# A spectral filter and a low-rank mixer on one core: two batches turned on TensorE, a split store, and small work moved between engines

## The chip, the core and the metric

The kernel runs on one core of a Trainium2 chip. Its engines work side by side, each through its own list in order: TensorE (PE in the profile) multiplies matrices and writes to PSUM, VectorE (DVE), ScalarE (ACT) and GpSimd (POOL) work on vectors, and SyncE (SP) only issues transfers. DVE and ACT can read PSUM[...]. Transfers between DRAM and on-chip memory run on 16 DMA engines; SP, ACT and POOL queue them. The metric is the device time of one execution in microseconds (us); lower is better.

## The reference

For each of 8 batches of 3136 tokens by 256 features the program filters along the tokens in the frequency domain, then mixes. It is, shortened:

```python
X = np.fft.rfft(x, axis=1)
y = np.fft.irfft(X * (filt_r + 1j * filt_i)[None], n=3136, axis=1)
h = y.transpose(0, 2, 1) @ U @ V               # rank 32, along the tokens
u = y + h.transpose(0, 2, 1)
out = u + np.maximum(u @ w_ch1, 0.0) @ w_ch2   # 256 -> 1024 -> 256
```

Inputs and outputs are f32; the kernel works in f16 and accumulates in f32.

## The kernel before

The length is split as 3136 = 64 x 49, so that the transform becomes small matrix products with constant matrices. **Stage 1** (`st1`) is 25 products of x with `wf`, a 64-point transform; its result goes to DRAM (`ct1`) and comes back regrouped as `a2` (eight tiles, k = 0 to 7, of 98 rows by 4 x 256). **Stage 2** is two matmuls of 512 columns for each k with `w2t`. Its result is multiplied by the filters, `fb` and `fc`, three element-wise products and one sum (`mul`, with `ta`, `tb`, `y`). **Stage 3** is two matmuls with `g3`; its result is evicted to `esb` and stored to DRAM (`ct2`). **Stage 4** (`stage4`) reads it back as `e2` in chunks of 8 of the 49 residues, with the low-rank term in 32 extra rows (`put_h`), and multiplies by `sv`; the result `ut` is the mixer's input, turned. `mm1` multiplies by the first weight `w1sb` (ReLU on ACT into a ring of 17 `h` tiles), `mm2_part` by the second, `w2sb`, and `residual` adds `ut` back.

From the main loop on the work is written as **groups** of 512 tokens, six for each batch, each of eight steps: a step has one `mm1` of the group and a quarter of a `mm2` of the group before, and stage 4 of the next group stands at steps 2 and 6. Everything else is placed by an order written out by hand: `plan` holds what follows a step, `early` what precedes it. `plan_mid` places stages 2 and 3 of the next batch, `plan_rest` its low-rank part and the loads of `e2`, `plan_st1` stage 1 of the batch after that. One PSUM bank (tag `e`) serves stage 3 there, and one pair of banks stage 2.

What lies ahead of the main loop is called the preamble here. Batch 0 cannot be hidden behind another, and so has its own form: `turned` (L295) computes stage 1 with x as the stationary operand, so that the result comes out turned, into `cm`, which is laid over `fc`; `turn_a2` (L358) turns it back on TensorE with eight transposes for each k, without DRAM. `mid_first` (L354) does stages 2 and 3 with **doubled matrices**: each half of a k takes two matmuls of 512 columns in stage 2 and two in stage 3, but one single product of 1024 columns, since real and imaginary parts stand twice. Of its 16 products four (L397, j = 7, 9, 12, 14) are GpSimd's, after a copy out of PSUM on ACT; twelve (L400) are DVE's. After it come the low-rank part (L416), all of stage 1 of batch 1 (L266), and stage 4 of group 0; `make_fa` (L541) then derives the operands `fa` (laid over `fb`) and `fc` for the three-product form. In batch 1 k = 1, 3 and 5 are multiplied by GpSimd (`pooled`, L636), in later batches k = 2 and 5.

Loads that change f32 to f16 are queued on POOL, in this order: U, x of batch 0, 21 filter pieces, V, the first weight, x of batch 1, the second weight. SP loads `wf` and `s4`, stores, and reads back. Within one queue a transfer that waits holds up all behind it. `keep_warm` issues matmuls whose result nobody reads.

## Time and profile before

| | |
|---|---|
| median of 8 runs | 556.46 us (555.63 to 561.68) |
| profiled execution, its own time | 556.53 us |
| span of its instructions | 554.7 us |
| TensorE busy | 515.5 us, 93% of the span |
| ACT, DVE, GpSimd busy | 390.8, 352.9, 282.6 us |
| mean granted TensorE clock | 0.982 of full speed |
| first product of batch 0 (L400) | 25.41 us |
| first `mm1` of batch 0 (L488) | 60.90 us |
| first `mm1` of batch 1 | 134.63 us |

In the profile, `L488 PE MATMUL` is an instruction of line 488 on TensorE; `out<-in` names tiles. In a list in order of time each line has start and length in us, engine, line, operation, operands and count, and in brackets the idle time of the engine before it with what ended it. A line of waits reads: who waited for whom, us in total, times, longest. The page's `PEclk` row has 40 equal slices of the span; its digits are tenths of the full TensorE clock.

### The profile page before, as it was taken

How to read it: one execution, taken by the hardware profiler on the slowest of the kernel's cores; microseconds unless marked ns; L12 is line 12 of the kernel's file. 1: busy time of each engine (PE TensorE's matmuls, PEld its weight loads, DVE VectorE, ACT ScalarE, POOL GpSimd, SP SyncE). 2: the span in 40 equal slices, each digit the busy share in tenths (PEclk: the TensorE clock that was granted, in tenths of full speed). 3: DMA queues.
4: the chain of work that ended last, by engine and by line, in shares of the span. 5: the costliest groups of instructions: out<-in, count | busy, mean ns of one | idle time of the engine just before them, and what ended most of it. 6: DMA issues, size and time to landing. Idle time of an engine off the chain costs nothing.

```text
span 554.7 us, 11638 instructions
## 1 busy us (share of the span) xinstructions
PE 515.5 (93%) x4491; PEld 374.4 (67%) x4491; DVE 352.9 (64%) x409; ACT 390.8 (70%) x684; POOL 282.6 (51%) x194
## 2 busy tenths in 40 slices
PE   4977599986999999999999999999999999999996
PEld 2634266664767777677776777777776777777775
DVE  6764776755756785758846785758746887643332
ACT  8566868774777688767777788677767677765663
POOL 5688279951893165915683185807563287300000
PEclk8799989999999999999999999999999999999999
DMA  9998886895779468775879469765654554333212
GB/s 191 159 158 176 235 161 184 211 225 135 180 186 248 126 179 196 171 194 151 193 219 220 123 173 229 166 201 154 182 170 123 141 166 121 106 113 115 96 77 87
DMA packets 85432, 92.06 MB, mean 166 GB/s; under 512 B 6741, under 2 KB 69416, under 8 KB 85376
## 3 DMA queue, kind: packets, MB, share of 16 engines
q1 hardware_dynamic: 67968, 75.12, 46.0%
q0 software_dynamic: 16960, 15.91, 19.2%
q8 instruction: 35, 0.57, 0.4%
q10 hardware_dynamic: 448, 0.28, 0.3%
q14 instruction: 21, 0.17, 0.1%
HBM read 57.42 MB, written 49.77 MB: 193 GB/s over the span
## 4 chain that ended last, share of the span: by engine, by line
PE 64%; POOL 5%; DVE 3%; ACT 2%; issue 1%; ACTq 0%; POOLq 0%; DVEq 0%
PE psum L521 24%; PE psum L488 23%; PE psum L352 3%; PE psum L344 3%; PE psum L497 3%; PE psum L477 3%; PE psum L266 2%; POOL y L634 2%; DVE tb L632 1%; PE psum L416 1%; POOL x L170 1%; POOL tb L632 1%; POOL ta L628 1%; POOL tb L630 1%; DVE ut L482 1%
## 5 line engine op out<-in xcount | busy, mean ns | idle before, releaser
L492 ACT ACTIVATE hring<-psum 128x512 f16<-128x512 f32 (+1 forms) x416 | 237.7, 576 | 102.3 <-PE psum L488 101.1
L488 PE MATMUL psum<-ut,w1sb 128*128 128x512 f16 (+1 forms) x832 | 240.9, 371 | 3.5 <-ACT hring L492 1.7
L521 PE MATMUL psum<-w2sb,hring 128*128 128x256 f16 x1536 | 230.7, 273 | 0.0
L634 POOL TENSOR_TENSOR y<-ta,tb 128x1024 f16<-128x1024 f16 x56 | 120.6, 2160 | 159.6 <-DVE tb L632 125.1
L521 PEld LDWEIGHTS <-hring 128*128 128x128 f16 x1536 | 143.3, 98 | 62.4 <-issue 2.6
L482 DVE CAST ut<-psum 128x512 f16<-128x512 f32 x96 | 71.0, 740 | 105.4 <-PE psum L477 85.9
L488 PEld LDWEIGHTS <-w1sb 128*128 128x128 f16 x832 | 104.7, 145 | 26.1 <-issue 9.5
L529 DVE COPY och<-psum 128x512 f32<-128x512 f32 x96 | 66.2, 689 | 47.6 <-PE psum L497 46.9
L326 ACT CAST esb<-psum 98x512 f16<-98x512 f32 x128 | 74.8, 587 | 22.1 <-PE psum L344 16.4
L273 ACT CAST asb<-psum 128x512 f16<-128x512 f32 x78 | 45.8, 589 | 14.0 <-PE psum L266 12.9
L628 DVE TENSOR_TENSOR ta<-psum,fb 128x1024 f16<-128x1024 f32 x41 | 49.9, 1218 | 8.9 <-PE psum L352 8.0
L497 PE MATMUL psum<-idn,ut 128*128 128x128 f16 x392 | 53.9, 219 | 0.0
L477 PEld LDWEIGHTS <-e 96*128 96x128 f16 x768 | 35.5, 98 | 24.7 <-issue 9.3
L630 DVE TENSOR_TENSOR tb<-psum,fc 64x1024 f16<-64x1024 f32 x41 | 50.3, 1226 | 0.9
L632 DVE TENSOR_TENSOR tb<-psum,fc 64x1024 f16<-64x1024 f32 x41 | 49.9, 1218 | 0.8
L477 PE MATMUL psum<-sv,e 96*128 96x64 f16 x768 | 38.4, 193 | 5.9 <-DMA e<-ct 3.1
L344 PE MATMUL psum<-y,g 128*98 128x512 f16 x105 | 39.9, 380 | 2.7 <-POOL y L634 1.2
L497 PEld LDWEIGHTS <-ut 128*128 128x128 f16 x392 | 38.4, 98 | 4.8
L352 PE MATMUL psum<-a,w2t 98*128 98x512 f16 x113 | 34.7, 383 | 3.4 <-DMA a<-ct 2.4
L628 POOL TENSOR_TENSOR ta<-pc,fb 128x1024 f16<-128x1024 f16 x15 | 32.4, 2159 | 10.2 <-ACT pc L638 10.1
L266 PE MATMUL psum<-x,wf 128*128 128x256 f16 x168 | 31.1, 272 | 4.2 <-DVE ut L482 1.8
L630 POOL TENSOR_TENSOR tb<-pc,fc 64x1024 f16<-64x1024 f16 x15 | 31.9, 2125 | 1.2
(93 smaller groups left out, 370.8 us busy)
## 6 DMA issues: line engine op xcount, KB each, us to landing
out_dram<-och SPq DMA_DIRECT2D x47, 512.0 KB
ct<-esb SPq DMA_DIRECT2D x64, 196.0 KB
x<-in_x_dram POOLq DMA_DIRECT2D x48, 256.0 KB, 7.9
e<-ct SPq DMA_DIRECT2D x48, 256.0 KB
a<-ct SPq DMA_DIRECT2D x56, 196.0 KB
ct<-asb SPq DMA_DIRECT2D x42, 256.0 KB
wf<-wf SPq DMA_DIRECT2D x3, 256.0 KB
w1sb<-in_moe_w_ch_dram POOLq DMA_DIRECT2D x1, 512.0 KB, 7.0
```

The costliest lines, as they stand in the source:

```text
L326: nc.scalar.copy(esb[b, k][:, 2 * half:2 * half + 2, :].rearrange("p s d -> p (s d)"), pe[0:98])
L477: nc.tensor.matmul(pu[:, 64 * i:64 * i + 64], e2[b, c][:, i, 128 * dh:128 * dh + 128], sv[:, 64 * r:64 * r + 64], start=(i == 0), stop=Tru ...
L482: nc.vector.tensor_copy(o, v)
L488: nc.tensor.matmul(ph[:, 0:n], w1sb[:, dh, :, t], gr.ut[:, dh, 0:n], start=(dh == 0), stop=(dh == 1))
L492: nc.scalar.activation(h[:, 0:n], ph[:, 0:n], RELU)
L497: nc.tensor.matmul(o[:, dh * 128:dh * 128 + 128], gr.ut[:, dh, t0:t0 + n], idn, start=False, stop=(dh == 1), skip_group_check=True)
L521: nc.tensor.matmul(o, gr.h[tt][:, i * 128:(i + 1) * 128], w2sb[:, tt, :], start=(tt == 0), stop=False, skip_group_check=True)
L529: nc.vector.tensor_copy(gr.och[:, 2 * y:2 * y + 2, :].rearrange("p j d -> p (j d)"), gr.pc)
L628: eng.tensor_mul(ta, p, va)
L630: eng.tensor_mul(tb[0:64], p[64:128], vb[64:128])
L632: eng.tensor_mul(tb[64:128], p[0:64], vb[0:64])
L634: nc.gpsimd.tensor_add(ys[k], ta, tb)
```

## The change

It has these parts.

- **Layout.** Only 49 + 15 + 49 = 113 rows are used where 128 were (`NZ`), `fb` is zeroed in rows 32 to 63 alone, on DVE, and `cm` has a tile of its own. `tb` becomes three fixed tiles with zeroed middle rows.
- **Constants.** `wf` is loaded at half width and spread on DVE by two multiplications with a 0/1 column. U is loaded by SP as f32. `s4` and `kr` follow the first store.
- **mid_first.** Fifteen products are DVE's, one (j = 11) GpSimd's. Stage 3 follows two j behind. The low-rank matmuls are spread over it, and `make_fc` for k = 4 to 7 runs on ACT in it.
- **The last store.** The store of k = 7 is cut in four by rows: 0-8 (SP) and 49-57 (ACT queue), on which chunk 0 of `e2` depends, then 8-49 and 57-98. Chunk 0 is loaded in three pieces.
- **Batch 1.** Its stage 1 is `turned` like batch 0's; k = 0 and 1 are turned back ahead of the main loop, k = 2 to 7 at steps 1, 3, 7, 11, 15, 17. k = 0 to 3 use the doubled matrices (`two_q`, `mul_q`, `three_q`), k = 4 to 7 the three products, all on DVE. Stage 3 of batch 1 ends at step 37 instead of 40.
- **GpSimd's queue.** After the filters: V, x of batch 1, the copy into `sv`, the first weight, the j = 11 product; the second weight waits for chunk 0 of `e2` (by a copy of one element) and is written in pieces of 256 elements into rows of 264. `make_fc` for k = 0 to 3 and `make_fa` are 49-row copies on GpSimd; `make_neg` is DVE's.
- **x.** Of batch 3 it is loaded at steps 30, 38, 43, 45.

```diff
-    wf = np.zeros((128, 25, 128))
+    wf = np.zeros((128, 25, 64))
     for h in range(2):
-        wf[h::2, 0:24, 64 * h:64 * h + 64] = t1[:, 24 * h:24 * h + 24]
-    wf[0:64, 24, 0:64] = t1[:, 48]
+        wf[h::2, 0:24] = t1[:, 24 * h:24 * h + 24]
+    wf[0:64, 24] = t1[:, 48]
+
+    pair = np.zeros((128, 2), np.float32)
+    pair[0::2, 0] = pair[1::2, 1] = 1.0
...
-    wf = cst.tile([128, 25, 128], F16, name="wf")
-    for c in range(4):
-        i = slice(8 * c, min(8 * c + 8, 25))
-        nc.sync.dma_start(wf[:, i], wf_d.rearrange("p (i m) -> p i m", m=128)[:, i])
+
+    usb = hflat[0:64, 0:2 * NR * RANK].bitcast(F32)
+    nc.sync.dma_start(usb, moe_U.rearrange("(q r) p -> q (r p)", q=NQ))
+    wfc = hflat[:, 6272:6272 + 1604]
+    nc.sync.dma_start(wfc, wf_d)
+    wf = cst.tile([128, 24, 128], F16, name="wf")
+    wl = cst.tile([64, 64], F16, name="wl")
...
-    zero = cst.tile([128, 64], F16, name="zero")
-    nc.vector.memset(zero, 0.0)
-    nc.vector.memset(fb[96:128], 0.0)
-    nc.scalar.copy(fb[32:64].rearrange("p s (k f) -> p (s k) f", f=64),
-                   free(zero, 32, 64, 0, [[0, NK * DM // 64], [1, 64]]))
-    nc.vector.memset(fc[:, 24:29, :], 0.0)
-    usb = hflat[0:64, 0:NR * RANK]
-    nc.gpsimd.dma_start(usb, moe_U.rearrange("(q r) p -> q (r p)", q=NQ))
+    nc.vector.memset(fb[32:64], 0.0)
+
+    cm = cst.tile([128, 7232], F16, name="cm")
+    nc.vector.memset(cm[:, 2 * SEQ:], 0.0)
...
+    ud = hflat[0:64, 3136:6272].rearrange("q (p c r) -> q p c r", c=2, r=NR)
+    for p, eng in ((0, nc.vector.tensor_copy), (16, nc.scalar.copy)):
+        eng(ud[:, p:p + 16], bass.AP(tensor=usb.tensor, offset=usb.offset + p,
+                                     ap=[list(usb.ap[0]), [1, 16], [0, 2], [RANK, NR]]))
+    for h in range(2):
+        nc.vector.tensor_scalar_mul(wf[:, :, 64 * h:64 * h + 64],
+                                    wfc[:, 0:1536].rearrange("p (i m) -> p i m", m=64),
+                                    wfc[:, 1600 + 2 * h:1602 + 2 * h].bitcast(F32))
+    nc.vector.tensor_copy(wl, wfc[0:64, 1536:1600])
+    tbs = [cst.tile([NZ, 4 * DM], F16, name=f"tb_{i}") for i in range(3)]
+    for t in tbs:
+        nc.vector.memset(t[32:64], 0.0)
...
+    def turn_back(k, tag, dst, eng):
+        z = bank(tag).bitcast(F16)
+        for i in range(4):
+            for hh in range(2):
+                nc.tensor.transpose(z[:, DM * i + 128 * hh:DM * i + 128 * hh + 128],
+                                    free(cm, 0, 128, SEQ * hh + 4 * k + i, [[32, 128]]), idn)
+        (nc.vector.tensor_copy if eng is nc.vector else nc.scalar.copy)(dst, z[0:98])
...
+    def store3(b, k, p0, p1, eng=nc.sync):
+        eng.dma_start(dram(ct2[b], (4 * k * 98 + p0) * DM, [[DM, p1 - p0], [98 * DM, 4], [1, DM]]),
+                      esb[b, k][p0:p1])
...
+    fa = fb
+
+    def make_fc(k, copy):
+        copy(fc[0:NR, 4 * k:4 * k + 4], fb[64:NZ, 4 * k:4 * k + 4])
+
+    def make_neg(k):
+        nc.vector.tensor_scalar_mul(fc[64:NZ, 4 * k:4 * k + 4], fb[64:NZ, 4 * k:4 * k + 4], -1.0)
+
+    def make_fa(k):
+        nc.gpsimd.tensor_copy(fa[64:NZ, 4 * k:4 * k + 4], fb[0:NR, 4 * k:4 * k + 4])
+        if k == 7:
+            nc.gpsimd.tensor_copy(fa[64:65, 31, :], fc[0:1, 31, :])
+            for p in (0, 64):
+                nc.gpsimd.memset(fc[p:p + 1, 31, :], 0.0)
...
+        ph = psum[:, 1, 0:DM]
+
+        def low_rank_part(k):
+            for i in range(4):
+                a = 4 * k + i
+                nc.tensor.matmul(ph[32 * i:32 * i + 32], uh[:, a, :], esb[0, k][:, i, :],
+                                 start=(k == 0), stop=(k == 7), skip_group_check=True)
+
+        whole = []
 
         def do3(j, uv):
             pe = bank("e0")
             stage3(pe, [(uv[:, 0], 2, 4), (uv[:, 1], 3, 5)], j == 15)
-            out3(0, j // 2, j % 2, pe)
-
-        for k in range(4):
+            while whole and j > 3:
+                low_rank_part(whole.pop(0))
+            k = j // 2
+            out3(0, k, j % 2, pe)
+            if ndone[0, k] == 2:
+                whole.append(k)
+                if k == 0:
+                    nc.sync.dma_start(sv[0:64], s4_d)
+                    nc.sync.dma_start(kr, kr_d)
+                if k == 6:
+                    load_e2(0, 0, 40, 0)
+                if k == 7:
+
+                    store3(0, 7, 0, 8)
+                    store3(0, 7, 49, 57, nc.scalar)
+                    load_e2(0, 0, 56, 40)
+                    load_e2(0, 0, 64, 56)
+                    store3(0, 7, 8, 49)
+                    store3(0, 7, 57, 98)
...
+        for k in range(2):
             turn_a2(k)
         for c in range(4):
             load_x(1, c)
-        nc.gpsimd.dma_start(w2sb, moe_w_ch2.rearrange("(cc t) e -> cc (t e)", t=8))
+        nc.gpsimd.tensor_copy(sv[64:96, :].rearrange("p (r q) -> p r q", q=NQ),
+                              vnat.rearrange("p (q r) -> p r q", q=64))
+        nc.gpsimd.dma_start(w1sb, moe_w_ch1.rearrange("(h dd) c -> dd h c", h=2))
...
-            fin = free(fb, 0, 128, 2 * j * DM, [[0, 2], [1, 2 * DM]])
-            if j in (7, 9, 12, 14):
-                pc = sb.tile([128, 2, 2 * DM], F16, tag="pc", bufs=2, name="pc")
-                nc.scalar.copy(pc, pz)
-                uv = sb.tile([128, 2, 2 * DM], F16, tag="y", bufs=3, name="uv")
+            fin = free(fb, 0, NZ, 2 * j * DM, [[0, 2], [1, 2 * DM]])
+            uv = sb.tile([NZ, 2, 2 * DM], F16, tag="y" if j == 11 else "ta", bufs=3, name="uv")
+            if j == 11:
+                pc = sb.tile([NZ, 2, 2 * DM], F16, tag="pc", bufs=2, name="pc")
+                nc.scalar.copy(pc, pz[0:NZ])
                 nc.gpsimd.tensor_mul(uv, pc, fin)
             else:
-                uv = sb.tile([128, 2, 2 * DM], F16, tag="ta", bufs=3, name="uv")
-                nc.vector.tensor_mul(uv, pz, fin)
-            if j < 4:
-                turn_a2(j + 4)
-            todo.append((j, uv))
-            if len(todo) > 3:
-                do3(*todo.pop(0))
-        while todo:
-            do3(*todo.pop(0))
-
-
-    h1 = {}
+                nc.vector.tensor_mul(uv, pz[0:NZ], fin)
+            if j in (6, 8, 10, 12):
+                make_fc(j // 2 + 1, nc.scalar.copy)
+            if j < 6:
+                turn_a2(j + 2)
+            todo.append((j + (4 if j == 11 else 2), j, uv))
+            for t in sorted(todo):
+                if t[0] <= j or j == 15:
+                    do3(*t[1:])
+                    todo.remove(t)
+        low_rank_part(7)
+        h1[0] = hp = sb.tile([128, DM], F16, tag="hp", bufs=1, name="hp")
+        nc.vector.tensor_copy(hp, ph)
...
     keep_warm(10)
-    u_hat()
+    turned(0, 0)
+    u_hat(0, 8)
+    keep_warm(2)
+    turned(0, 1)
+    u_hat(16)
+    keep_warm(2)
+    for c in (2, 3):
+        turned(0, c)
+    u_hat(24)
+    mid_first()
+    gens = {}
+
+    def step1(b):
+        if b not in gens:
+            gens[b] = st1(b)
+        next(gens[b])
+
+    low_rank_end(0)
+    put_h(0, 0)
+    nc.gpsimd.tensor_copy(w2sb[64:65, 0, DM:DM + 1], e2[0, 0][64:65, 0, 0:1])
+    nc.gpsimd.dma_start(w2sb[:, :, 0:DM], moe_w_ch2.rearrange("(cc t) e -> cc t e", t=8))
+    for k in range(4):
+        make_fc(k, nc.gpsimd.tensor_copy)
     for c in range(4):
-        turned(c)
-        keep_warm(2)
-    nc.sync.dma_start(sv[0:64], s4_d)
-    nc.sync.dma_start(kr, kr_d)
-    mid_first()
-    load_e2(0, 0)
-    load_e2(0, 1)
-    nc.gpsimd.tensor_copy(sv[64:96, :].rearrange("p (r q) -> p r q", q=NQ),
-                          vnat.rearrange("p (q r) -> p r q", q=64))
-    low_rank(0)
-    for n, _ in enumerate(st1(1)):
-        if n == 3:
-            low_rank_end(0)
-        if n == 6:
-            put_h(0, 0)
-    load_e2(0, 2)
-    load_e2(0, 6)
-    keep_warm(6)
-    stage4(groups[0], 0)
-    stage4(groups[0], 1)
+        turned(1, c)
     for c in (1, 2, 6):
-        put_h(0, c)
-    make_fa(0)
-    make_fa(1)
+        load_e2(0, c)
+    a2q = {}
+
+    def turn_1(k, tag, eng):
+        a2q[k] = sb.tile([98, 4 * DM], F16, tag="a2", bufs=4, name="a2")
+        turn_back(k, tag, a2q[k], eng)
+
+    turn_1(0, "f0", nc.vector)
+    turn_1(1, "f0", nc.scalar)
+    for k in range(4, 8):
+        make_neg(k)
+    keep_warm(4)
+    for dh in range(2):
+        stage4(groups[0], dh)
+    put_h(0, 1)
...
+        def two_q(k, half):
+            box[k, half] = [psum[:, 5:7, :]]
+            for f in range(2):
+                stage2(psum[:, 5 + f], w2t[:, 128 * f:128 * f + 128],
+                       w2t[:, 256 + 128 * f:384 + 128 * f],
+                       a2[k][:, 2 * half * DM:2 * half * DM + 2 * DM], (k, half) == (7, 1))
+
+        def mul_q(k, half):
+            uv = sb.tile([NZ, 2, 2 * DM], F16, tag="ta", bufs=3, name="uv")
+            nc.vector.tensor_mul(uv, box[k, half][0][0:NZ],
+                                 free(fb, 0, NZ, (4 * k + 2 * half) * DM, [[0, 2], [1, 2 * DM]]))
+            box[k, half].append(uv)
+
+        def three_q(k, half):
+            uv = box[k, half][1]
+            pe = bank("e")
+            stage3(pe, [(uv[:, 0], 2, 4), (uv[:, 1], 3, 5)], (k, half) == (7, 1))
+            out3(b, k, half, pe)
+
         end = 0
-        for k in range(8):
+        if b == 1:
+
+            for j, q in enumerate((4, 6, 7, 8, 10, 11, 12, 14)):
+                at(q, two_q, j // 2, j % 2)
+                early[q + 1].append((mul_q, (j // 2, j % 2)))
+                at(q + 2, three_q, j // 2, j % 2)
+        else:
+            for k in range(3):
+                at(later(s, -6 if b == 2 else -9), fetch, k)
+        for k in range(4 if b == 1 else 0, 8):
+            if b > 1 and k + 3 < 8:
+                at(s, fetch, k + 3)
             at(s, two, k)
-            if k + 3 < 8:
-                at(s, fetch, k + 3)
             if k in on_pool:
...
-    at(1, make_fa, 2)
-    at(3, make_fa, 3)
+    for n, c in ((9, 2), (9, 6)):
+        at(n, put_h, 0, c)
+    for n, k, eng in ((1, 2, nc.vector), (3, 3, nc.vector), (7, 4, nc.scalar), (11, 5, nc.vector),
+                      (15, 6, nc.scalar), (17, 7, nc.vector)):
+        at(n, turn_1, k, "e", eng)
 
     def x_after(b):
 
         for c in range(4):
-            load_x(b, c, groups[0].h[3] if c == 0 else None)
-
-    at(4, x_after, 2)
+            load_x(b, c, groups[0].h[1] if c == 0 else None)
+
+    at(2, x_after, 2)
+    for c in range(4):
+        at((30, 38, 43, 45)[c], load_x, 3, c)
+    for k in range(4):
+        at(k, make_neg, k)
+    for k in range(4, 8):
+        at(2 * k - 4, make_fa, k)
+    for k in range(4):
+        at(2 * k + 18, make_fa, k)
     for b in range(1, NB):
         if b == 2:
-            plan_st1(b, 12, (0, 1, 3, 4, 5, 7))
+            plan_st1(b, 14, (0, 1, 3, 4, 5, 7))
         elif b > 2:
             plan_st1(b, later(start[b - 1], -60))
-        m = later(start[b - 1], (5, -9, -12)[min(b, 3) - 1])
-        z = plan_mid(b, m, (2, 5) if b > 1 else (1, 3, 5))
+        m = later(start[b - 1], (16, -9, -12)[min(b, 3) - 1])
+        z = plan_mid(b, m, (2, 5) if b > 1 else ())
```

## The prediction

> **What bounds the kernel now.** I read the page's engine rows first, then the stretches by batch, then waits and instructions in order of time inside the two stretches that are not full.
>
> ```profile
> span 554.7 us, 11638 instructions
> PE 515.5 (93%) x4491; PEld 374.4 (67%) x4491; DVE 352.9 (64%) x409; ACT 390.8 (70%) x684; POOL 282.6 (51%) x194
> PEclk8799989999999999999999999999999999999999
> ```
>
> TensorE (PE) is the bound overall, but its clock is cut early on. Busy time by stretch (columns: length, then PE, PEld, DVE, ACT, POOL busy, clock, DMA share, GB/s):
>
> ```profile
> 0.00:60.90 60.90, 42.74 (x313) 25.88 (x313) 36.69 (x45) 40.20 (x47) 39.94 (x50) 0.89 0.96 179
> 60.90:71.17 10.27, 6.52 (x41) 3.29 (x37) 9.24 (x17) 8.12 (x10) 4.65 (x8) 0.83 0.82 210
> 71.17:134.63 63.46, 55.12 (x464) 38.74 (x463) 40.61 (x45) 43.33 (x78) 42.75 (x26) 0.97 0.80 183
> 134.63:199.00 64.37, 62.88 (x562) 46.34 (x561) 42.60 (x49) 48.51 (x92) 35.47 (x22) 1.00 0.70 179
> 258.49:554.70 296.21, 289.13 (x2603) 216.59 (x2601) 182.16 (x210) 206.16 (x378) 126.03 (x69) 1.00 0.54 151
> ```
>
> The cuts are where the first `mm1` of a batch starts. From 134.63 on PE is 98% busy, and the change leaves that work alone. What can move is the preamble (60.9) and batch 0's window (73.7, of which PE is busy 61.6). Their landmarks, in order of time:
>
> ```profile
> 25.41 3.48 DVE L400 TENSOR_TENSOR uv<-psum,fb 128x1024 f16<-128x1024 f32 x3
> 39.88 0.66 PE L344 MATMUL psum<-uv,g 128*98 128x512 f16 x2 [3.28 <-POOL uv L397]
> 50.27 0.31 SPq L329 DMA_DIRECT2D ct<-esb  x1
> 53.85 1.10 SPq L438 DMA_DIRECT2D e<-ct  x2
> 60.90 0.41 PE L488 MATMUL psum<-ut,w1sb 128*128 128x512 f16 x1
> 68.00:72.00 4.00, 3.77 (x16) 1.64 (x16) 3.63 (x8) 2.07 (x4) 3.49 (x6) 0.50 0.98 203
> ```
>
> The first product is at 25.4, one of PE's three waits for GpSimd products is 3.28, the last `esb` leaves at 50.27, and SyncE may read it back only at 53.85: a store needs 3.6 us to land. The last line is again a stretch: with the clock at 0.50, 16 matmuls fill PE for 3.77 us, so a busy PE there is half a PE. In batch 0's window the waits are
>
> ```profile
> PE psum L477 <- DMA e<-ct: 3.1, 1, 3.1
> PE psum L352 <- DMA a<-ct: 2.4, 2, 1.5
> ```
>
> the first at its end (batch 1's first `e`), the second where batch 1's stage 2 waits for stage 1 to come back from DRAM.
>
> **What the skill says.** "DMA: Bandwidth & Descriptors", section "Why a DMA increments its semaphore by 16 and not by 1": a transfer queued by SyncE runs on the largest number of engines up to 16 that divides its rows, always the lowest-numbered ones, each writing one completion. The trace agrees on the number: SyncE's queue has 4,368 packets of 4 bytes, exactly 14 for each of its 120 98-row transfers and 16 for the 168 others. "TensorE: Matmul & The Clock Gate", "What's actually happening": after an idle window of some 3.4 us the clock halves. The trace agrees: half rate for 6.8 us from 67.6. "VectorE: DVE Perf Modes", "The perf-mode tier table": a product from PSUM runs at 1x; here 1.22 us for 1,024 elements, on 128 as on 64 partitions, so 113 partitions gain nothing.
>
> **S1, start to first product.** U comes as f32 by SyncE (+0.2 MB), `wf` at half width (-0.4), `s4` after the first store (-0.4): 0.6 MB less before the last x. At the 189 GB/s of the first 20 us that is 3.1 us; x lands at 16.5 instead of 19.6. The lag from there to the product was 5.8. Removed: ACT's 7.0 us zero fill. Added on DVE: two scaled copies of `wf`, three memsets, about 2.6 us, under the x loads. First product 22.0.
>
> **S2, mid_first.** Before: 25.41 to 50.24, with 4.6 of PE waits for GpSimd. After: DVE has 15 products x 1.22 + a 0.69 copy = 19.0; ACT has 6 turns x 1.01 + 16 evictions x 0.59 + 4 `make_fc` at about 1.0 (half of 1.89 for twice the columns) + 1.01 = 20.6, beginning 1.5 earlier. The one GpSimd product waits for the 6.97 us `sv` copy but has four slots. I take 21.5: last `esb` at L = 43.5. x of batch 1 lands by 42.5 (shifted as above, `s4` in, `w1sb` out), in time.
>
> **S3, L to the first mm1.** Before 10.7, with stage 1 of batch 1 in it. After: low-rank end and `put_h` 2.6; seven DVE evictions of batch 1's turn x 0.69 4.7; turn back 0.6 and copy 0.7, with latencies 1.5; four `make_neg` x 0.37 (half of 0.69) 1.5; `ut` 0.75; second stage 4 0.35. Sum 11.4: first `mm1` at 54.9, 6.0 earlier.
>
> **S4, batch 0's window.** PE was busy 61.6, of which 3.4 is the half clock; 58.2 at full rate. Added: six turns back x 8 transposes x 0.0725 = 3.5, and 16 more 512-column matmuls x 0.217 = 3.5 by the doubled matrices. Gone: the wait for `a`, and the wait for `e` at the end, since the last stage 3 stands at step 37 instead of 40. DVE has 8 products of the doubled kind and 12 others for batch 1, 20 x 1.22 = 24.4, where it had 15 (18.3), since three k were GpSimd's; it loses the eight 0.69 passes of `make_fa` (5.5), so it stays near 51 of 73, off the bound unless the `two`/`mul` pair shares its PSUM buffer step by step, when each product (1.22) must fit into a step (about 1.3). GpSimd drops nine products of 2.13 (19.2) for twelve 49-row copies, a kind that the trace lacks: between 1.1 (half of a two-input pass of 2.16) and 2.3 (6.97 for 3,136 columns), I take 2.2. Four of them stand ahead of x of batch 2, which is issued by L + 19.5, lands 7 to 10 later, and is first used at step 15, near L + 38; the others ahead of the adds `y`, from step 20 on. One PSUM bank serves turns back and stage 3; PE waits for the eviction (0.6 to 1.0) if it is late. With 4.0 of such gaps: 69.2. Bounds: 66 to 73.
>
> **S5, a new wait.** The store of k = 7 is cut into rows 0-8, 49-57 and twice 41 rows, so that `e` of chunk 0 can return early. 41 has no divisor up to 16: both go to one engine. 2 x 164 packets of 512 bytes x 27 ns (their median now) = 8.9 us. Issued at L + 3.5 to 4.2, after the small stores land, first packet about L + 4.9, end L + 13.8, landing L + 14.5; the second weight's packets, let go by `e` of chunk 0, may add 64 x 60 ns = 3.8. SyncE holds `e` of chunk 1 until then, and it takes 2.6: L + 17.1 to 20.6. PE wants it at step 2, about L + 14.4. Stall 2.7 to 6.2; behind it in PE's order stand all of `mm1`, stage 2 and stage 3, and the clock may fall (up to 3.4). Partly S4's gaps are the same time: I add 4.5. Bounds 0 (several engines) to 15.
>
> **S6.** Batch 1: the same plan, x of batch 3 issued at four fixed steps; -0.5. Moves costed at nothing: the first weight is issued behind the `sv` copy, at about 39, and lands 7.0 later (its time now), 9 us before 54.9; the second, in 1 KB pieces, takes 1,024 packets x 60 ns / 16 = 3.8 (before, 128 of 4,096 bytes x 322 ns / 16 = 2.6), issued near L + 6 = 49.5, landed by 60, and `mm2` starts eight steps after 54.9, near 65. If that cover went, each microsecond would stop PE. `put_h` of chunks 2 and 6 and the fc copies keep 10 us of slack and more. Rest 355.7.
>
> **Sum.** 54.9 + 69.2 + 4.5 + 63.9 + 355.7 = 548.2, and the profiled run has 1.8 outside its span (556.53 against 554.7); its time is 0.07 above the median of 556.46. Forecast 550.
>
> **Rivals.** A: the two 41-row stores spread, or `e` is not needed so soon; then no S5: 545.5. For it: the trace shows no few-engine store by SyncE at all. B: the preamble wins only half, ACT and DVE alternating behind PE's order in mid_first as they did (22 us for 12 products), and S5 comes: 555, no change. C: slower. One engine serves the 41-row stores at the contended packet time, 48 ns (95th percentile now): 15.7 + 3.8 of packets, `e` of chunk 1 at L + 27.7, a stall of 13.3 and a half clock of 3.4 less the shared gap: 561. It decides from an arrival at about L + 25. Against it: DMA is then less busy than at 40 us. That the change does not do what it says is excluded: the instruction order of the changed kernel has it.
>
> **Chances.** Forecast 0.45 (own range 546 to 554), A 0.25, B 0.17, C 0.13. A measurement tells 0.5%: faster below 553.7, slower above 559.2. Faster 0.43 + 0.25 + 0.05 = 0.73, same 0.02 + 0.12 = 0.14, slower 0.13. Range 542 (A with S4 at its lower end) to 559.5.
>
> **What would show it.** S1: first 113-row product near 22. S2: last `esb` near 43.5, no GpSimd wait on PE over 1. S3: first `mm1` near 55. S4: no wait for `a`, stage 4 of batch 1 not waiting. S5: stage 4 waiting for `e` in the first group, 3 to 6 us, with a long tail of single 512-byte packets. Wrong if x of batch 1 is late at its turn, or if ACT's evictions stop PE in every step.

## The result and the profile after

The changed kernel takes 563.98 us (median of 11 runs, 558.40 to 568.50), beside 556.68 for the kernel before on the same chip. The ratio is 1.0124, interval 1.0095 to 1.0153: slower by 1.2%, where the forecast was faster by 1.2%. The profiled execution took 564.19 us with a span of 562.4. The page of the changed kernel, its engine rows:

```profile
span 562.4 us, 11825 instructions
PE 521.4 (93%) x4590; PEld 379.8 (68%) x4590; DVE 362.3 (64%) x422; ACT 380.3 (68%) x683; POOL 261.6 (47%) x193
PEclk9898699998999999999999999999999999999999
```

PE has only 5.9 us more busy time; 7.7 us were added to the span. The fifth digit of the clock is a 6, and that is the place. The stretches of the changed kernel, cut at the first `mm1`, at the second group of batch 0, and at the first `mm1` of batches 1 and 2 (length, then PE, PEld, DVE, ACT, POOL busy, clock, DMA share, GB/s):

```profile
0.00:54.82 54.82, 41.47 (x347) 25.75 (x348) 42.99 (x58) 32.72 (x48) 38.24 (x51) 0.94 0.96 171
54.82:76.15 21.33, 9.13 (x71) 5.83 (x68) 7.26 (x11) 6.55 (x11) 9.84 (x16) 0.76 0.61 109
76.15:141.98 65.83, 59.18 (x498) 41.84 (x497) 45.56 (x51) 41.53 (x75) 18.45 (x16) 0.97 0.60 144
141.98:206.47 64.49, 62.95 (x562) 46.35 (x561) 42.61 (x49) 48.54 (x92) 35.49 (x22) 1.00 0.72 181
266.16:562.40 296.24, 289.36 (x2602) 216.42 (x2600) 182.13 (x210) 206.38 (x378) 125.66 (x69) 1.00 0.53 151
```

The preamble is 6.1 shorter (54.82 for 60.90), as forecast. Batch 1 and all behind it are as before. Everything that was lost, 13.4 us, is batch 0's window: 87.16 in place of 73.73. Most of that is in its first group, 21.33 long with PE busy for 9.13. In the changed kernel's list in order of time (start, length; SPq and ACTq are the issues of SyncE and ACT) the landmarks are:

```profile
20.28 1.23 DVE L454 TENSOR_TENSOR uv<-psum,fb 113x1024 f16<-113x1024 f32 x1 [0.74 <-ACT a L326]
43.00 0.28 ACTq L347 DMA_DIRECT2D ct<-esb  x1
46.58 0.29 SPq L495 DMA_DIRECT2D e<-ct  x1
46.92 0.29 SPq L347 DMA_DIRECT2D ct<-esb  x1
47.90 3.75 SPq L495 DMA_DIRECT2D e<-ct  x2
51.70 2.73 SPq L347 DMA_DIRECT2D ct<-esb  x2
54.82 0.41 PE L546 MATMUL psum<-ut,w1sb 128*128 128x512 f16 x1
61.34 1.41 SPq L495 DMA_DIRECT2D e<-ct  x2
68.59 0.59 PE L535 MATMUL psum<-sv,e 96*128 96x64 f16 x8 [11.05 <-DMA e<-ct]
```

The first product is at 20.28 (before, 25.41) and the last `esb` leaves by 43.0 (before, 50.27); up to here the change does what it says. Then read SyncE's issues downward. The 40-row load of chunk 0 (46.58) waits at the head of the queue for the store of k = 4, and the small store stands behind it (46.92); the two loads at 47.90, the rest of chunk 0, wait for the store of k = 6 and for the small stores; the two 41-row stores are issued at 51.70, and `e` of chunk 1 is let go at 61.34, 9.6 us after them. PE sat idle for 11.05 before stage 4 that reads it. The waits of PE in the window:

```profile
PE psum L535 <- DMA e<-ct: 11.1, 1, 11.1
PE psum L370 <- DMA a<-ct: 2.6, 1, 2.6
PE psum L276 <- DVE ut L540: 1.8, 1, 1.8
```

The first is new. The second is the old wait for `a` in another place (batch 2's stage 2, 128.4). The third was there before as well; in the kernel before its line is

```profile
PE psum L266 <- DVE ut L482: 1.8, 1, 1.8
```

How the stores ran is seen in two short stretches of the changed kernel, columns as above:

```profile
50.00:52.00 2.00, 1.18 (x16) 1.06 (x16) 1.23 (x4) 0.62 (x1) 0.91 (x1) 1.00 1.33 201
54.00:57.00 3.00, 1.84 (x21) 1.39 (x21) 1.56 (x3) 1.47 (x3) 0.00 (x0) 1.00 0.10 27
```

Up to 52 the second weight fills the engines (the share adds up packets whose times overlap, so that it can pass 1). From 54 on the share is 0.10, of which one packet of another queue makes 0.03, and one engine of 16 is 0.06: the two stores crawl on one engine, at 22 GB/s without that packet, while the other fifteen have next to nothing to do. Each of the two has one completion that comes with its data, at 57.40 and 61.27.

Put together, the window's 87.16 are the stall of 11.05, other idle time of 7.8, PE's work of 65.2 at full clock, and 3.1 lost to half clock (from 61.1 to 71.4, of which PE worked 2.8, and 3.4 more from 129.4).

### The profile page after: what moved, and what is told of

It is laid out like the page before. It is cut to its first block, busy times and chain, and to the rows that moved or that the text cites. A ratio compares the mean times of both kernels' runs of the same rounds, so it can differ in the third digit from the quotient of the medians.

```text
span 562.4 us, 11825 instructions
## 1 busy us (share of the span) xinstructions
PE 521.4 (93%) x4590; PEld 379.8 (68%) x4590; DVE 362.3 (64%) x422; ACT 380.3 (68%) x683; POOL 261.6 (47%) x193
## 4 chain that ended last, share of the span: by engine, by line
PE 63%; POOL 5%; DVE 3%; ACT 2%; issue 1%; ACTq 0%; POOLq 0%; DVEq 0%
PE psum L579 23%; PE psum L546 23%; PE psum L370 3%; PE psum L362 3%; PE psum L555 3%; PE psum L535 3%; PE psum L276 2%; POOL y L696 2%; DVE tb L694 1%; PE psum L473 1%; POOL x L178 1%; POOL ta L690 1%; POOL tb L694 1%; POOL tb L692 1%; DVE ut L540 1%
## 5 line engine op out<-in xcount | busy, mean ns | idle before, releaser
L696 POOL TENSOR_TENSOR y<-ta,tb 113x1024 f16<-113x1024 f16 x52 | 111.9, 2157 | 187.5 <-DVE tb L694 151.8
L690 DVE TENSOR_TENSOR ta<-psum,fb 113x1024 f16<-113x1024 f32 x40 | 48.7, 1218 | 13.5 <-PE psum L370 10.8
L280 ACT CAST asb<-psum 128x512 f16<-128x512 f32 x72 | 42.4, 590 | 14.5 <-PE psum L276 13.0
L535 PE MATMUL psum<-sv,e 96*128 96x64 f16 x768 | 38.3, 193 | 13.3 <-DMA e<-ct 11.1
L692 DVE TENSOR_TENSOR tb<-psum,fc 49x1024 f16<-49x1024 f32 x40 | 49.1, 1226 | 1.1
L694 DVE TENSOR_TENSOR tb<-psum,fc 49x1024 f16<-49x1024 f32 x40 | 48.7, 1219 | 1.1
L370 PE MATMUL psum<-a,w2t 98*128 98x512 f16 x121 | 37.5, 387 | 5.8 <-DMA a<-ct 2.6
L362 PE MATMUL psum<-y,g 113*98 113x512 f16 x97 | 37.0, 382 | 2.1 <-ACT esb L340 1.0
L178 POOL DMA_DIRECT2D x<-in_x_dram x48 | 30.7, 653 | 1.3 <-POOLq L843 0.8
L690 POOL TENSOR_TENSOR ta<-pc,fb 113x1024 f16<-113x1024 f16 x12 | 26.0, 2165 | 9.9 <-ACT pc L700 9.9
L276 PE MATMUL psum<-x,wf 128*128 128x256 f16 x144 | 27.7, 274 | 2.1 <-DVE ut L540 1.8
```

What stands on the lines that cost most here:

```text
L535: nc.tensor.matmul(pu[:, 64 * i:64 * i + 64], e2[b, c][:, i, 128 * dh:128 * dh + 128], sv[:, 64 * r:64 * r + 64], start=(i == 0), stop=Tru ...
L690: eng.tensor_mul(ta, p[0:NZ], va)
L692: eng.tensor_mul(tb[0:NR], p[64:NZ], vb[64:NZ])
L694: eng.tensor_mul(tb[64:NZ], p[0:NR], vb[0:NR])
L696: nc.gpsimd.tensor_add(ys[k], ta, tb)
```

## The experiments

In the expectations T1 is that the 41-row stores make the wait, by their one engine and, as a second half, by SyncE's queue order ahead of them; T2 is that the loads of x of batch 2 make it long; T3 is the rival to both. Ratios are to the kernel before, on the same chip, with their intervals.

**Even stores.** Each 41-row store becomes one of 32 rows and one of 9.

```diff
-                    store3(0, 7, 8, 49)
-                    store3(0, 7, 57, 98)
+                    for p0, p1 in ((8, 40), (40, 49), (57, 89), (89, 98)):
+                        store3(0, 7, p0, p1)
```

> The changed kernel with one edit: each of the two 41-row stores of k = 7 is cut into 32 and 9 rows. Theory T1 (one DMA engine carries both 41-row stores, and chunk 1 of e waits for them): the four stores, issued from about 51.7, land by 56 instead of 61.3; chunk 1 of e is issued at 56, ahead of most of batch 2's x, and arrives near 59; the stall of 11.05 us at stage 4 falls to about 2, and the half clock behind it goes: 11 to 14 us less than the changed kernel, some 550. Rival T2 (the load itself is slow because x of batch 2 is on the same engines, wherever it starts): the load still takes 7, arrives at 63, stall 5.5: 5 to 6 us less. Rival T3 (the loss is the work added to batch 0's window, the stall only stands where other waits would stand): under 3 us less.

Measured: 554.74 us, ratio 0.9961 (0.9939 to 0.9984), span 552.5. In its list in order of time:

```profile
50.35 1.45 SPq L347 DMA_DIRECT2D ct<-esb  x4
53.06 1.09 SPq L495 DMA_DIRECT2D e<-ct  x2
```

`e` of chunk 1 is issued 2.7 us after the first of the four stores, not 9.6, and PE doesn't wait for it at all: the first group takes 10.03.

```profile
54.13:64.16 10.03, 7.79 (x71) 5.24 (x67) 7.26 (x11) 6.55 (x11) 6.93 (x11) 1.00 0.89 150
```

By medians 9.2 us came back from a change of shape in two stores, so that without this shape there is no slowdown: the first half of T1 holds, and T3 falls.

**The 40-row load moved.** The load that held SyncE's queue is issued behind the small stores; the stores keep 41 rows.

```diff
-                if k == 6:
-                    load_e2(0, 0, 40, 0)
...
                     store3(0, 7, 49, 57, nc.scalar)
+                    load_e2(0, 0, 40, 0)
                     load_e2(0, 0, 56, 40)
```

> The changed kernel with one edit: SyncE's 40-row load of chunk 0 of e stands behind the small stores of k = 7 instead of ahead of them. T1 in its second half (SyncE's queue was blocked from 42.4 to 46.6 by that load, which waited for the store of k = 4): the small store goes out at 43.0 instead of 46.9, the 41-row stores at 47.5 to 48, they land near 57 on their one engine, chunk 1 of e arrives at 60 to 63; stall 3 to 6 instead of 11: 6 to 10 us less than the changed kernel. If the queue's order does not matter (the stores would be as late anyway, because the engines are full until 46): under 2 us less. T3: under 2 us less.

Measured: 562.29 us, ratio 1.0106 (1.0050 to 1.0162). In its list in order of time:

```profile
48.22 5.92 SPq L347 DMA_DIRECT2D ct<-esb  x2
61.04 1.15 SPq L494 DMA_DIRECT2D e<-ct  x2
67.36 0.59 PE L534 MATMUL psum<-sv,e 96*128 96x64 f16 x8 [8.01 <-DMA e<-ct]
```

The stores are issued 3.5 us earlier, and the issue of the two then takes 5.92 in place of 2.73; `e` is let go at 61.04, as late as before. The single packets in the trace show what stood in the way. The loads of chunk 0 are ahead of the stores in SyncE's queue, and the first packet of the stores starts at 52.92, just when the last packet of these loads ends. (In the changed kernel both times are 52.75.) The loads are slow beside the second weight, whose packets run until 52.76. So the 40-row load delays the issue, but the engine was not free any earlier: the time is not to be told from the changed kernel's, and the second half of T1 falls.

**Both together.** Even stores, and the load moved.

> Both edits: 32 and 9 rows instead of 41, and the 40-row load behind the small stores. T1: all four stores land by 52 to 53, chunk 1 of e arrives by 56, no stall at step 2; first mm1 near 54.8 as before, batch 0's window near 70 instead of 87.2: 543 to 547, below the kernel before. T3: not below 556.

Measured: 554.55 us, ratio 0.9965 (0.9943 to 0.9988): as with even stores alone, and well above what was expected. SyncE's issues in its list:

```profile
46.96 2.02 SPq L347 DMA_DIRECT2D ct<-esb  x4
53.12 1.09 SPq L494 DMA_DIRECT2D e<-ct  x2
```

The four stores are issued 3.4 us earlier than with even stores alone, and `e` is let go no earlier (53.12 for 53.06). Their first packet starts at 49.94, and the second weight's packets run until 52.49: even stores do move beside the weight, but slowly. The stretch from the first `mm1` to batch 1 of this kernel, and PE's longest waits in it:

```profile
54.53:129.09 74.56, 65.42 (x566) 46.51 (x563) 52.91 (x62) 47.88 (x85) 28.37 (x31) 1.00 0.67 152
```

```profile
PE psum L370 <- DMA a<-ct: 2.5, 1, 2.5
PE psum L276 <- DVE ut L539: 1.8, 1, 1.8
PE psum L362 <- DVE uv L718: 1.3, 1, 1.3
```

PE's work is 65.4, at full clock. The idle time in the window is 9.1 us, and this kernel has no stall for `e`: the window is still 0.8 longer than before the change.

**x of batch 2 later.** The changed kernel, with x of batch 2 let go by the fourth `h` at step 4 in place of the second at step 2.

```diff
-            load_x(b, c, groups[0].h[1] if c == 0 else None)
+            load_x(b, c, groups[0].h[3] if c == 0 else None)
-    at(2, x_after, 2)
+    at(4, x_after, 2)
```

> The changed kernel with x of batch 2 released by the fourth mm1 at step 4, as in the kernel before, instead of by the second at step 2. Stage 4 of the next group stands at step 2, so x is then not on the engines while chunk 1 of e is loaded. T1: the stores still land at 61.3, so the load is issued at 61.3; T2: alone it takes 2.6 instead of 7.1 and arrives near 64; stall 6.5 instead of 11, and a shorter half clock: 4 to 7 us less than the changed kernel. If x is not what slows the load: under 2 us less.

Measured: 560.69 us, ratio 1.0077 (1.0032 to 1.0122). In its list in order of time:

```profile
61.49 1.09 SPq L495 DMA_DIRECT2D e<-ct  x2
65.29 0.59 PE L535 MATMUL psum<-sv,e 96*128 96x64 f16 x8 [5.72 <-DMA e<-ct]
```

From the issue of `e` to PE it is 3.8 us, where the changed kernel had 7.25. The loads of x of batch 2 (57.9 to 71.2 there) do make the wait longer, and T2 holds for that part. But the clock was at half from 54.3 to 71.3 here, and the window is 86.19 for 87.16, so that this moves the profiled span by 0.4 only. That profile is of the slowest of the seven executions; by medians 3.3 us came back, but the intervals of the two kernels overlap.

**The second weight in whole rows.** The changed kernel, with `w2sb` written in rows of 4 KB in place of 1 KB pieces.

```diff
-    w2sb = cst.tile([128, 8, DM + 8], F16, name="w2sb")
+    w2all = cst.tile([128, 8 * DM + 8], F16, name="w2sb")
+    w2sb = w2all[:, 0:8 * DM].rearrange("p (t e) -> p t e", t=8)
...
```

> The changed kernel with the second weight written in whole rows of 4 KB again instead of 1,024 pieces. The packets of the two 41-row stores did not move while the second weight's packets ran (about 47.5 to 52.5). If the pieces lengthen that phase (3.8 against 2.6 us of packets on each engine), the stores start and land 1 to 2 us earlier: 1 to 3 us less than the changed kernel. If the source (1 MB of f32) sets the phase's length, no difference: within 1 us.

Measured: 566.39 us (4 runs), ratio 1.0213 (1.0167 to 1.0258). The weight lands 6.2 us after its issue, where the pieces took 6.9; PE still waits 8.0 for `e`. The pieces are not what made the change slow. Why the whole rows come out slower still is open. The profile, of the fastest of the four executions, shows no wait that they add. Its clock was at half from 39.3 to 49.6, and the first `mm1` is at 56.77; but this began ahead of the weight's issue at 47.80, so that the edit did not cause it.

**Stage 1 of batch 1 through DRAM.** On the kernel with even stores and the load moved, `st1(1)` and `load_a2` take the place of `turned` and the turns back, and its copies out of PSUM go to ACT and DVE in turn.

```diff
-    for c in range(4):
-        turned(1, c)
+    for _ in st1(1):
+        pass
...
-    turn_1(0, "f0", nc.vector)
-    turn_1(1, "f0", nc.scalar)
+    for k in range(3):
+        a2q[k] = load_a2(1, k)
...
```

> The version with both edits, with batch 1's stage 1 as in the kernel before (products of 256 columns, results to DRAM, a2 loaded back) instead of turned, in the same place, with copies out of PSUM on ACT and DVE in turn. PE loses the 64 transposes (4.6 us, 3.5 of them in batch 0's window) and waits instead for a2: its stores are queued behind the loads of e and land near 57 to 60, the first a2 near 62, wanted at step 4 near 60. If the turn is worth its transposes: 0 to 4 us slower than with both edits. If not (the transposes cost more than the return from DRAM): 1 to 4 us faster.

Measured: 558.74 us (5 runs), ratio 1.0086 (1.0050 to 1.0123), 4.2 us above the kernel it is to be compared with by medians, 1.2% by the ratios. In its list in order of time:

```profile
49.77 6.15 SPq L284 DMA_DIRECT2D ct<-asb  x6
56.02 0.93 SPq L293 DMA_DIRECT2D ct<-al  x1
57.00 1.72 SPq L494 DMA_DIRECT2D e<-ct  x2
```

Seven stores stand ahead of `e` of chunk 1 in SyncE's queue: it leaves at 57.00 in place of 53.12, PE waits 4.1 for it and 5.3 in two waits for `a`. PE's work in the window, with what half clock lost taken off, is 61.8 in place of 65.4: the transposes cost what S4 said, and the way through DRAM costs more. That holds for this order of the queue alone. The expectation had these stores behind the loads of `e`, but they stand ahead of them; the other order was not tried.

**Three products for every k of batch 1.** On the same kernel, no doubled matrices in batch 1; k = 1, 3 and 5 go to GpSimd. In this kernel the negated part of `fc` (`make_neg`) is formed for k = 2 and 3 from rows that `make_fa` has already replaced: those two filters have other values, with the same instructions and sizes.

```diff
-        if b == 1:
+        if b == -1:
...
-        for k in range(4 if b == 1 else 0, 8):
+        for k in range(8):
...
-        z = plan_mid(b, m, (2, 5) if b > 1 else ())
+        z = plan_mid(b, m, (2, 5) if b > 1 else (1, 3, 5))
...
```

> The version with both edits, without the doubled matrices in batch 1: all eight k by three products, k = 1, 3 and 5 on GpSimd after an ACT copy as in the kernel before, the operand copies of GpSimd at steps 0 to 6. Stage 3 then ends at step 40 instead of 37. If the added matmuls (16 x 0.217 = 3.5 us) cost what S4 says, batch 0's window is 3.5 shorter in PE work; but the first e of batch 1 is issued three steps later and PE waits for it at the window's end as before (3.1). I expect within 2 us of the version with both edits; clearly slower (over 3) would say that the doubled matrices are worth their matmuls, clearly faster (over 3) that they are the wrong trade.

Measured: 560.57 us (4 runs), ratio 1.0109 (1.0059 to 1.0160), 6.0 above by medians. This does not price the doubled matrices as a whole. All eight copies of `make_fa` now stand at steps 0 to 6, and the edit makes a wait of its own:

```profile
69.73 1.23 DVE L379 TENSOR_SCALAR fc<-fb 49x1024 f16<-49x1024 f16 x1 [4.97 <-POOL fb L382]
71.77 0.58 PE L545 MATMUL psum<-ut,w1sb 128*128 128x512 f16 x1 [6.07 <-DVE ut L539]
```

DVE waits 4.97 for GpSimd's copy with the eviction of `ut` behind it, and PE 6.07 for that. Besides, the first `mm1` is 3.4 later in this profile (57.90), with a half clock from 40.3 to 50.5 in the preamble, which the edit leaves alone. One price can be read: PE's work in the window, with what half clock lost taken off, is 61.7 in place of 65.4, so that the doubled matrices cost 3.7 of PE, near the 3.5 of S4. What they save in waits stays open.

**Stage 1 of batch 2 earlier.** Even stores, the load moved, stage 1 of batch 2 planned from step 12 in place of 14, and its `a` fetched two steps sooner. This and the next three kernels look at the 9.1 us of idle time.

```diff
-            plan_st1(b, 14, (0, 1, 3, 4, 5, 7))
+            plan_st1(b, 12, (0, 1, 3, 4, 5, 7))
...
-                at(later(s, -6 if b == 2 else -9), fetch, k)
+                at(later(s, -8 if b == 2 else -9), fetch, k)
```

> The version with both edits, and stage 1 of batch 2 planned from step 12 instead of 14 (it then ends three steps earlier, at 28), with its first three a2 loads at step 31 instead of 33. Theory: what is left of the loss against the step S4 (74.6 us of batch 0's window where 69.2 was expected) is mostly the wait for a of batch 2 (2.46 us) and the half clock behind it (3.4 us at half rate, 1.7 lost); both go: 3 to 4 us less than with both edits. Rival: stage 1 so early meets x of batch 2 that has not landed or ACT's fullest steps, and PE waits there: no gain, or slower.

Measured: 551.62 us, ratio 0.9921 (0.9900 to 0.9941). The wait for `a` is gone and the window's idle time is 6.15 in place of 9.14. In this profile the clock was at half for 6.8 us (53.0 to 59.8) in the first group, which takes 2.8 of it back (window 74.03).

**One eviction on ACT.** As above, and the second `ut` of batch 1's first group is evicted by ACT.

```diff
-        (nc.scalar.copy if gr is groups[0] and dh else nc.vector.tensor_copy)(o, v)
+        act = dh and (gr is groups[0] or gr is groups[6])
+        (nc.scalar.copy if act else nc.vector.tensor_copy)(o, v)
```

> Even stores, the 40-row load moved and stage 1 of batch 2 two steps earlier, and besides the second ut eviction of batch 1's first group moved from DVE to ACT. In the run before, PE waits 1.8 us at the end of batch 0's window for that eviction: it shares its PSUM bank with the next step of stage 1, and DVE does a product of 1.2 first, while ACT is idle for 2.5 us. Theory: the wait goes (-1.8), and the half clock of 3.4 us that follows it goes in part (-1 at most): about 549 (ratio 0.988). Rival: the next product or ACT's own activations take the wait over, and nothing changes: 551.5 (0.992).

Measured: 549.00 us, ratio 0.9858 (0.9810 to 0.9905). The window of this kernel:

```profile
53.98:125.26 71.28, 65.41 (x567) 46.27 (x563) 51.52 (x60) 48.50 (x86) 28.34 (x31) 1.00 0.66 152
```

The wait for `ut` falls from 1.8 to 0.4. But the idle time falls by only 0.3, from 6.15 to 5.87: the longest wait of stage 3 for `uv` goes from 0.5 to 1.3. The rest of the 2.75 by which this window is shorter is the half clock at the start of the other one, ahead of anything this edit touches. The intervals of the two kernels touch as well, so that the expectation's rival, other waits taking this one over, is not excluded. No half clock follows here at the window's end, but the kernel below with all products on DVE still has the wait of 1.8 and none either. 71.28 with 5.87 idle is the nearest to the forecast's 69.2 with 4.0.

**Four more fillers** between the turn of batch 1 and its first turn back, on that kernel.

```diff
+    keep_warm(4)
     turn_1(0, "f0", nc.vector)
```

> As the kernel with that ut eviction on ACT, with four more 512-column filler matmuls between the turn of batch 1 and its first turn back, where PE waits 1.1 us twice. Theory of the clock: the half clock of 3.4 to 6.8 us that some executions show between 44 and 60 us comes from the waits of 0.5 to 1.1 us there; with the wait filled it comes less often, 0.5 to 1.5 us less than without the fillers. Rival: it makes no difference, or the fillers (0.87 us of PE) delay the first mm1 by up to 0.9.

Measured: 548.97 us, ratio 0.9848 (0.9805 to 0.9890): no difference from the kernel without them, though the first `mm1` of its profile is 1.1 later (55.08). The half clock at 43.9 to 47.3 stands ahead of them, and is still there.

**The GpSimd product undone.** Even stores, the load moved, and all 16 products of `mid_first` on DVE.

```diff
-            if j == 11:
+            if j == -1:
...
-            todo.append((j + (4 if j == 11 else 2), j, uv))
+            todo.append((j + 2, j, uv))
```

> Even stores and the 40-row load moved, and all 16 products of batch 0's middle stages on DVE: the one product of GpSimd (2.13 us, with a copy of 0.58 to 1.0 on ACT ahead of it) is undone. DVE has 1.2 us more and is the engine that PE waits for at the end of that stretch, ACT about 1 less. If DVE bounds the stretch, the first mm1 comes 1 us later than with the GpSimd product, about 55.5 in place of 54.5, and the time is about 555.5 (ratio 0.998). If ACT bounds it, it is 0.5 to 1 earlier: 554 (0.995).

Measured: 553.27 us, ratio 0.9940 (0.9917 to 0.9964), beside 0.9965 (0.9943 to 0.9988) with the product on GpSimd. The last `esb` leaves at 41.7 in place of 42.8, 1.1 earlier. The times fit with ACT as the bound, but the intervals overlap.

**All that helped, together.** Even stores, load moved, stage 1 earlier, the eviction on ACT, no GpSimd product.

> Even stores, the 40-row load moved, stage 1 of batch 2 two steps earlier, the second ut eviction of batch 1's first group on ACT, and all 16 products of batch 0's middle stages on DVE. If the parts add: the last esb leaves 1.1 us earlier than with the GpSimd product, so about 548 (ratio 0.984), a little under the 0.9858 that the same kernel with the GpSimd product had. Rival: SyncE's loads of e then come no earlier and PE waits for them in front of the first mm1: no difference, 549.

Measured: 548.42 us, ratio 0.9878 (0.9841 to 0.9915): not to be told from the kernel with the GpSimd product. Its first `mm1` is at 53.11, but the clock is at half from 53.0 to 56.4 there. By the ratios either one is 1.2 to 1.4% faster than the kernel before, and about 2.5% faster than the changed kernel.

## Why the prediction was wrong

**S1 held, a little too small.** First product at 20.28, predicted 22.0 (its own terms, 16.5 and 5.8, give 22.3); x of batch 0 landed at 14.94, predicted 16.5.

**S2 held.** 22.7 from there to the last `esb` in place of 21.5; its end, L, at 42.97 (predicted 43.5). The one GpSimd product brings no long wait for PE, but the run without it ends 1.1 sooner.

**S3 held.** 11.85 in place of 11.4 (seven times 0.69 is 4.8, not 4.7); first `mm1` at 54.82, predicted 54.9.

**S4: the work was right, the gaps were not.** PE's work in the window is 65.2, as worked out; with even stores and the load moved it is 65.4. GpSimd's 49-row copies took 0.995 each (four in 3.98), where I had said between 1.1 and 2.3. The gaps were to be 4.0. They are 7.8 in the changed kernel beside the stall, and 9.1 where there is no stall. I had written that the wait for `a` goes; it only passed from batch 1 to batch 2, whose stage 1 now ends three steps later: its last rows land at 124.0, and PE waits 2.56. And I hadn't priced the wait for `ut` at the end of the window, 1.8 in both kernels. The wait for `a` was worth 3.0 of gaps (9.14 to 6.15). Without the wait for `ut` they are 5.87, 0.3 less, since other waits took most of it over.

**S5 is the step that failed.** The mechanism was named: two 41-row stores on one engine, SyncE holding `e` of chunk 1 behind them, PE stopped at step 2. Its size was 4.5; it measured 11.05, and 1.4 more of slow clock at its end. Three terms were put too low.

*The issue.* The stores were to be issued at L + 3.5 to 4.2 and were at L + 8.7. The 40-row load of chunk 0 stood at the head of SyncE's queue until the store of k = 4 had landed, 9.75 us after its issue (36.67 to 46.42), so that the small store behind it left only at L + 3.95. That step was in the diff, and I did not time it. The small store then took 4.4 to land.

*The start on the engine.* From issue to first packet I had at most 1.4. In the changed kernel it is 1.05. But the run with the load moved shows that the issue wasn't decisive alone: there it is 4.7, since the loads of chunk 0, ahead in SyncE's queue, kept the engine until 52.92. I had priced the second weight as 3.8 on the stores themselves; by 52.37 its packets had ended in the changed kernel, and if it cost anything there, it was through those loads and the small store. (With 3.8 my terms add to L + 20.9, not 20.6.) From 52.75 the 328 packets took 8.2, for which I had 8.9. The stores landed at L + 18.3 in place of L + 14.5.

*The load.* It took 7.1 in place of 2.6. x of batch 2 was on the engines; in the run with x later it landed 3.7 after its issue. And 2.6 was too low for quiet engines too: no load of a whole chunk of `e` in the kernel before landed in less than 3.37.

Sum: L + 25.5, predicted L + 17.1 to 20.6.

**One engine for 41 rows.** "DMA: Bandwidth & Descriptors", section "Why a DMA increments its semaphore by 16 and not by 1", from which I had read one engine for 41 rows, holds here: a DMA share of 0.10 where one engine is 0.06 and another queue's packet 0.03, one late completion for each store, and the slowdown gone with 32 + 9 rows. That rival A's first half, stores that spread, is thus excluded.

**The clock.** The prediction took the half clock from 67.6 as agreeing with the Trainium skill, "TensorE: Matmul & The Clock Gate", "What's actually happening", by which the clock halves after an idle window of some 3.4 us. The length agrees, twice 3.4. The idle window does not: ahead of 67.6 the kernel before has

```profile
62.00:67.00 5.00, 3.05 (x19) 1.63 (x19) 4.65 (x8) 4.71 (x6) 0.48 (x2) 1.00 0.71 196
```

with PE busy for 3.05 of 5 us and no wait over 1.5. In the changed kernel a half clock began at 44.1, and in the 3.4 us ahead of it PE was busy for 2.4 and waited at most 0.5 at once. So S5's 3.4 of slow clock after a long wait came (10.2 of half clock, 1.4 lost), but a long wait is not needed for it, and the prediction had no price for such pieces in its sum.

**S6 held**: batch 1 64.49 (predicted 63.9), the rest 355.95 (predicted 355.7).

**The sum.** Against 548.2 the span is 14.2 longer: S5 with its clock 7.9, S4's gaps 3.8, a half clock at 129.4 1.7, S6 and the rest 0.8.

**The rivals.** C gave 561 with an arrival of `e` at L + 27.7 and a stall of 13.3, deciding from L + 25. The arrival was L + 25.5 and the stall 11.05, so C is the one that came. But it came with another cause: not slower packets (328 in 8.2 us, 25 ns each, where the forecast had 27), but a late start and a slow load. A's case without S5 could be tried, with even stores: 554.7, not 545.5. A fails by S4's gaps and the clock: that kernel's window has 9.6 idle, for which S4 had 4.0, and loses 2.8 to half clock. B's half preamble didn't come.

I gave C 0.13 because I took its packet price as the only way to so late an arrival, while each of three other terms in the same sum (issue, start on the engine, load) had been put at its quiet value.

## What to carry to other kernels

A store that a later load waits for should have a row count that spreads over the engines: here 41 rows on one engine cost about 9 us of the program, and with 32 + 9 rows PE did not wait for the load at all. Where a transfer is queued behind a wait, time the whole queue from the store that ends the wait, and price each transfer by what else is on the engines then. When a wait is removed from one batch, look for the next batch's same wait: here it needed two steps more lead.

## What the runs showed of the hardware

- In the four kernels with 41-row stores the first packet of these stores started within 0.01 us of the end of the last packet of the loads ahead of them in SyncE's queue: at 52.75 (changed kernel), 52.92 (load moved), 53.37 (x later) and 53.86 (whole rows). Issued 3.5 us earlier (48.22 for 51.70), they let `e` go only 0.3 earlier, and the issue of the two took 5.92 in place of 2.73.
- The second weight's packets, from another queue, ended near these times too (52.37, 52.76, 53.21, 53.65), but they do not stop stores as such: in the kernel with both edits packets of the even stores moved from 49.94 on, and the weight's until 52.49. How much the weight lengthens the loads was not tried.
- `make_fc`, a copy of 49 rows by 1,024 in f16, took 0.995 us on GpSimd (four in 3.98), 1.04 on ACT.
- The store of k = 4 landed 9.75 us after its issue, with loads of x and of the first weight on the engines; with even stores the last ones and the wake of SyncE together took 2.7, and 6.2 with the 40-row load moved as well, where they were issued while the second weight was loading.
- Half clock came in pieces of 3.4, 6.8, 10.2, 17.1 and 20.5 us. Between 39 and 76 us it adds up to 13.7 (changed kernel) to 23.9 (whole rows) in the six kernels whose PE stalls there for 4 us or more, and to 3.4 to 6.8 in the other seven changed ones. In the run with x later it began at 54.3 and in the run with the load moved at 53.5, 5 to 6 us ahead of the stall for `e`, so the stall alone doesn't explain it. In nine of the thirteen changed kernels a piece of 3.4 began between 42.7 and 44.9, with PE busy for 1.6 to 2.4 of the 3.4 us ahead and no wait of 0.6 or more.
